# Another order for a hand-scheduled kernel: first loads on SyncE's queue, first weights on ScalarE's, and the rest of the instruction order searched anew

## The chip, the cores and the metric

The kernel runs on one core of a Trainium2 chip. The metric is the device time of one execution in microseconds (us). A "fast" run is one within 1.5% of the fastest run of the same kernel. Engines are named as the profile names them: PE is TensorE's matmuls, PEld its weight loads, DVE is VectorE, ACT is ScalarE, POOL is GpSimd, SP is SyncE, which here only issues DMAs. "L1085" is line 1085 of the kernel.

## The reference, cut to what matters

Two branches share x (2048 rows, 640 columns) and are mixed by a gate:

```python
def _A_ref(x, wq, wk, wv, wo, beta):      # 32 heads of 20, four segments of 512 rows
    q, k, v = heads(x @ wq), heads(x @ wk), heads(x @ wv)
    phi = lambda t: jnp.where(t > 0, t + 1.0, jnp.exp(t))
    for s in range(4):
        p = softmax(qs @ ks.T * scale + causal_mask)
        a_dot = p @ vs
        a_mem = (phi(qs) @ M) / (phi(qs) @ z + 1e-06)
        outs.append(g * a_mem + (1.0 - g) * a_dot)
        M, z = M + phi(ks).T @ vs, z + phi(ks).sum()
    return concat(outs) @ wo
def _B_ref(x, w_r, w_i):                  # spectral filter: rfft2, times W, irfft2
    return irfft2(rfft2(x) * (w_r + 1j * w_i))
g = sigmoid((x * gate_w).sum(-1, keepdims=True))
return g * a + (1 - g) * b
```

(The head reshapes and the loop's set-up are cut.) The Fourier transforms are matmuls with tables in the kernel, so TensorE carries both branches.

## The kernel before: what the change and the argument touch

The kernel builds a list of operations. A constant named ORDER then says in which order they are issued and on which engine each one goes. Every entry is twice the number of an operation, plus one if the operation runs on its second choice of engine:

```python
def schedule(self, pools, order, nsem=56):
    ops = self.ops
    queue = {e: [] for e in self.eng}
    for v in order:
        o = ops[v // 2]
        o.eng = list(o.alts)[v % 2]
        queue[o.eng].append(o)
    ...
ORDER = (
    47, 0, 90, 26, 74, 23, 2, 4, 37, 24, 6, 8, 28, 10, 12, 72, 14, 16, 30, 18, 20, 178, ...   # 2328 entries
```

So each engine has one fixed queue. An entry whose input is late holds up all that stand behind it on that engine, needed or not (one case, shown below, cost TensorE 2.15 us). The loads at the front are DMAs on the queues of SyncE or ScalarE; `EARLY` names those that may go on either:

```python
queues = ("sp", "act") if name in self.EARLY else (queue,)
```

The feature map phi is two VectorE operations between SBUF tiles, at L1084 and L1085 of the profile:

```python
fmax = lambda e: e.tensor_scalar(dst(), qsl(), 0.0, 1.0, ALU.max, ALU.add)
fmin = lambda e: e.tensor_tensor(dst(), dst(), et.ap(0, [1, L]), ALU.min)
```

The causal mask is GpSimd's (`affine_select`, L1284). The spectral product is read out of PSUM by VectorE (`W_mul`, Pt, L1439), and what follows it, an addition between SBUF tiles (`W_add`, Yt, L1444), may go on VectorE or GpSimd:

```python
def either(self, fn, n, r, w, prio, name="", after=()):
    return self.Sc.op({"dve": (fn, 67 + 0.52 * n, 68.0), "pool": (fn, 120 + 1.95 * n, 50.0)}, ..., lock=True)
```

In this kernel TensorE writes its results to PSUM, and another engine reads them out of there into SBUF. Such a read is called an evacuation below; TensorE waits for it before it writes the same bank of PSUM again.

TensorE works in three tilings: whole (128 x 128), in 32-column pieces and in small tiles for the scores (qkp). A change from one to another is called a change of mode.

The softmax here doesn't subtract the row's maximum and nothing guards it: scores larger than these inputs give would overflow.

## Time and profile before

| | before |
|---|---|
| median of 3 runs | 244.76 us (243.39 to 249.08) |
| span of the profiled run (an execution of its own, 246.77 us) | 244.7 us |
| TensorE busy | 94% of the span |
| VectorE / ScalarE / GpSimd busy | 81% / 81% / 68% |
| matmuls | 4361 (the trace holds 4347 of them) |

A row of the view of instruction groups reads: line, engine, operation, output<-input, size, count; then busy us in total and the mean of one in ns; then the idle time before them and its cause. This is a row of before that also belongs here, the second half of phi for q:

```profile
L1085 DVE TENSOR_TENSOR phq<-phq,et 128x512 bf16<-128x512 bf16 x15 | 6.7, 456 | 0.0
```

Keep its mean of 456 ns. The shortest of the 15 takes 407 ns and eleven of them at most 421, so in before most of them run undisturbed.

### The profile page before, as it was taken

The page shows a single profiled execution, that of the slowest core. Times are in us where ns is not written, and L with a number is a line of the kernel's source. Part 1 is how long each engine was busy: PE and PEld are TensorE (multiplying, and loading weights), DVE is VectorE, ACT ScalarE, POOL GpSimd, SP SyncE. Part 2 cuts the span into 40 slices and gives each one's busy share as a digit, 9 for nine tenths or more (in the row PEclk, how much of TensorE's full clock was granted, in tenths as well). Part 3 has the DMA queues.
Part 4 walks back from the last instruction along what each step waited for, and adds up shares of the span by engine and source line. Part 5 has one row for each costly group of instructions (what it writes and reads, how often), then busy time and mean ns, then how long its engine had stood idle before and what let it go on. Part 6 is the DMA issues. An engine that isn't in the chain of part 4 may idle for free.

```text
span 244.7 us, 10242 instructions
## 1 busy us (share of the span) xinstructions
PE 229.2 (94%) x4347; PEld 141.3 (58%) x4361; DVE 197.3 (81%) x481; ACT 199.3 (81%) x241; POOL 166.5 (68%) x297
## 2 busy tenths in 40 slices
PE   7699999999989999999889999899989999899994
PEld 2476566765556565555546555455545556467794
DVE  0379998879899996898899798998988878635563
ACT  2089688889899999999889979999899978388730
POOL 8514259447959956938964999877899867459730
PEclk9999999999999999999999999999999999599999
DMA  7999859993998775494688571264676995722123
GB/s 174 297 348 206 198 165 175 288 195 100 169 285 175 169 220 147 100 240 89 224 211 250 151 233 50 99 175 138 183 221 198 237 180 101 112 54 86 56 85 108
DMA packets 58928, 42.17 MB, mean 172 GB/s; under 512 B 30020, under 2 KB 55172, under 8 KB 58884
## 3 DMA queue, kind: packets, MB, share of 16 engines
q1 hardware_dynamic: 56100, 39.72, 66.4%
q10 hardware_dynamic: 2784, 1.81, 2.9%
q8 instruction: 34, 0.56, 1.0%
q14 instruction: 10, 0.08, 0.1%
HBM read 23.32 MB, written 12.30 MB: 146 GB/s over the span
## 4 chain that ended last, share of the span: by engine, by line
PE 59%; DVE 14%; DMA 10%; ACT 9%; SPq 3%; issue 2%; ACTq 0%; DVEq 0%
PE psum L514 53%; PE psum L512 7%; ACT ex L1263 6%; DMA xT<-in_A_x_dram 3%; DMA pkn<-phk 2%; SPq L548 2%; DMA r<-r_scr 2%; DVE Pt L1439 2%; DMA qk_scr<-qu 2%; DMA r_scr<-rc 2%; SPq L546 1%; DVE G L1485 1%; DVE phk L1085 1%; DVE oU L1526 1%; ACT et L1072 1%
## 5 line engine op out<-in xcount | busy, mean ns | idle before, releaser
L1284 POOL TENSOR_SCALAR_AFFINE_SELECT ex<-ex 128x256 bf16<-128x256 bf16 (+2 forms) x224 | 122.1, 567 | 41.1 <-ACT ex L1263 37.7
L1263 ACT ACTIVATE ex<-psum 128x2048 bf16<-128x2048 f32 (+4 forms) x92 | 138.7, 1508 | 13.9 <-PE psum L514 12.0
L514 PE MATMUL psum<-qkp 20*64 20x64 bf16 (+5 forms) x1280 | 32.7, 272 | 2.2 <-ACT ex L1263 1.7
L514 PE MATMUL psum<-xT,wk 128*128 128x256 bf16 (+1 forms) x280 | 34.1, 276 | 0.2 <-issue 0.2
L514 PE MATMUL psum<-wv,xT 128*32 128x321 bf16 (+3 forms) x400 | 30.1, 301 | 0.6 <-DVE va L1115 0.3
L514 PE MATMUL psum<-xT,wq 128*128 128x512 bf16 (+1 forms) x121 | 27.5, 396 | 2.6 <-DMA xT<-in_A_x_dram 2.0
L1439 DVE TENSOR_TENSOR Pt<-psum,Wt 128x642 bf16<-128x642 f32 x32 | 25.5, 821 | 2.3 <-PE psum L514 2.1
L514 PEld LDWEIGHTS psum<-qkp 20*64 20x64 bf16 x1280 | 13.5, 103 | 19.5 <-ACT ex L1263 13.6
L514 PEld LDWEIGHTS psum<-xT,wk 128*128 128x128 bf16 (+1 forms) x280 | 20.1, 99 | 6.4 <-issue 0.8
L512 PE MATMUL psum<-wo,oU 128*32 128x320 bf16 x480 | 23.5, 319 | 0.0
L906 POOL TENSOR_TENSOR xsb<-xf 128x320 bf16<-128x320 bf16 (+2 forms) x12 | 9.3, 777 | 17.7 <-DVE xsb L906 13.3
L525 DVE CAST ot<-psum 128x320 bf16<-128x320 f32 x21 | 10.1, 491 | 12.6 <-PE psum L512 10.1
L514 PEld LDWEIGHTS psum<-wv,xT 128*32 128x32 bf16 (+1 forms) x400 | 14.3, 96 | 8.4 <-issue 3.1
L514 PE MATMUL psum<-big,Ac 128*128 128x160 bf16 (+2 forms) x96 | 18.1, 258 | 0.7 <-DVE Pt L1439 0.3
L1115 DVE TENSOR_TENSOR va<-psum,ebx 128x320 bf16<-128x320 f32 x32 | 15.2, 484 | 4.3 <-ACT gate L1113 2.1
L514 PE MATMUL psum<-big,Cp 128*128 128x321 bf16 (+1 forms) x96 | 18.0, 302 | 0.2 <-DVE G L1485 0.2
L514 PE MATMUL psum<-ex,va 128*32 128x64 bf16 (+3 forms) x576 | 17.4, 256 | 0.7 <-DVE dn L1152 0.3
L1485 DVE TENSOR_TENSOR G<-eo,psum 128x320 bf16<-128x320 f32 x32 | 14.7, 482 | 3.6 <-PE psum L514 2.6
L514 PEld LDWEIGHTS psum<-ex,va 128*32 128x32 bf16 x576 | 11.1, 96 | 9.7 <-POOL ex L1284 3.4
L514 PE MATMUL psum<-tt,Yt 128*128 128x256 bf16 (+1 forms) x96 | 16.4, 275 | 0.2
L1072 ACT ACTIVATE et<-qu 128x512 bf16<-128x512 bf16 x25 | 15.6, 629 | 0.1
L512 PEld LDWEIGHTS psum<-wo,oU 128*32 128x32 bf16 x480 | 12.6, 101 | 5.3 <-issue 1.3
(99 smaller groups left out, 393.5 us busy)
## 6 DMA issues: line engine op xcount, KB each, us to landing
qkp<-qk_scr SPq DMA_DIRECT2D x28, 160.0 KB
tt<-tab_tt SPq DMA_DIRECT2D x8, 512.0 KB, 4.3
qk_scr<-qu SPq DMA_DIRECT2D x12, 256.0 KB, 3.1
u_scr<-ub SPq DMA_DIRECT2D x12, 256.0 KB, 3.8
xsb<-in_A_x_dram SPq DMA_DIRECT2D x6, 320.0 KB, 6.3
oU<-u_scr SPq DMA_DIRECT2D x15, 128.0 KB, 2.7
out_dram<-ot SPq DMA_DIRECT2D x12, 160.0 KB
Wt<-in_B_w_r_dram SPq DMA_DIRECT2D x16, 80.2 KB, 2.6
```

Of the source, the lines that this page charges most:

```text
L512: h = e.matmul(dst, wt, r_, start=st, stop=sp_, **{**kw, "tile_position": (0, q), "skip_group_check": True})
L514: h = e.matmul(o_, l_, r_, start=st, stop=sp_, **kw)
L525: alts["dve"] = (lambda e: e.tensor_copy(dst(), src()), 67 + 1.04 * n, 68.0)
L546: return e.dma_start_transpose(d_, s_)
L548: return e.dma_start(d_, s_)
L906: self.either(lambda e, dst=dst, src=src, d0=d0, n=n, op=op: e.tensor_tensor(xs.ap(o + dst, [D, 2], [1, n]), xf.ap(src + d0, [321, 2], [1, ...
L1072: self.one("act", lambda e: e.activation(et.ap(0, [1, L]), qsl(), ACT.Exp), L, [qb], [b("et", pi_)], late, name="phi_exp")
L1115: self.one("dve", lambda e: e.tensor_tensor(va.ap(i * H * VW + h0 * VW, [VW, nh], [1, DH]), self.ps(bank, 0, [DH, nh], [1, DH]), self.ebx. ...
L1263: self.one("act", lambda e, d=d, q=q: e.activation(self.ex.ap(*d), self.ps(bank, *q), ACT.Exp, scale=SC), n, [bank], [self.exb(s, 2 * pr + ...
L1284: self.one("pool", lambda e: e.affine_select(self.ex.ap(e0 + d0, [1280, 4], [1, n], np_=np_), self.ex.ap(e0 + s0, [1280, 4], [1, n], np_=np_),
L1439: self.one("dve", lambda e, ri=ri, Pt=Pt, Wt=Wt, wo_=wo_, bank=bank: e.tensor_tensor(Pt.ap(ri * 322, [644, 2], [1, KD]), self.ps(bank, 0, ...
L1485: self.one("dve", lambda e, q=q, n2=n2, bank=bank, eo=eo: e.tensor_tensor(self.G.ap(n2 * D + 639 * q, [1 - 2 * q, 320]), eo.ap(q, [1, 320] ...
```

## The change

The intent: put the first transposed chunks of x at the head of SyncE's queue with nothing on ScalarE's queue to compete, put the first weights on ScalarE's, and search the order of everything for a short time from scratch with measured durations of the transfers and of the ports. The diff touches no operation. Its core (the other lines of ORDER are cut; 2202 of the 2328 operations change their place in the list, half of them by six places or more, and 122 operations change engine or queue):

```diff
-    EARLY = ("ld_wqa", "ld_wka", "ld_wqb", "ld_wkb", "ld_wv", "ld_x", "ld_fcat", "ld_big", "ld_beta", "ld_gw", "ld_hm")
+    EARLY = ("ld_wqa", "ld_wka")
-        ... ("xT", 131072): (1260.0, 900.0, 16), ("xT", 262144): (1800.0, 1600.0, 16),
+        ... ("xT", 131072): (1240.0, 1300.0, 16), ("xT", 262144): (1700.0, 2300.0, 16),
     ORDER = (
-        47, 0, 90, 26, 74, 23, 2, 4, 37, 24, 6, 8, 28, 10, 12, 72, 14, 16, 30, 18, 20, 178, 64, 35, 202, ...
+        23, 0, 72, 28, 2, 4, 6, 26, 8, 10, 12, 76, 74, 36, 14, 46, 16, 24, 18, 30, 90, 44, 178, 64, 34, ...
```

In words: ScalarE's queue, which held a block of x (47), the first wq (23), beta (37), the rest of wk (35), another block of x and the gate column, keeps the first wq alone. SyncE's queue is now the transposed chunks 1-2 (28), chunk 0 (26), beta (36), a block of x (46), the first wk (24), the transposed chunks 3-4 (30), a block of x (44), the rest of wk (34). One of ten dummy matmuls that warm TensorE up moves behind the first wk work.

## The prediction

> **What bounds the kernel now.** I read the busy totals first, then the slices, then the timeline of TensorE wherever it was idle.
>
> ```profile
> span 244.7 us, 10242 instructions
> PE 229.2 (94%) x4347; PEld 141.3 (58%) x4361; DVE 197.3 (81%) x481; ACT 199.3 (81%) x241; POOL 166.5 (68%) x297
> ...
> PE   7699999999989999999889999899989999899994
> ```
>
> TensorE has work in flight for 229.2 of 244.7 us, so an order can win at most the 15.5 us of gaps, plus whatever is lost inside the busy share. The window table puts 3.3 us of the gaps before 12 us, 3.2 after 235 us (the last stores, which no order removes) and the other 9 in between, mostly pieces of 0.2 to 0.5 us. Two places are larger. The first is in the start:
>
> ```profile
> start us, us, engine line op out<-in xcount [idle before <-releaser]
> 4.69 1.06 PE L514 MATMUL psum<-G 128*128 128x512 bf16 x2
> 5.70 1.05 PE L514 MATMUL psum<-xT,wq 128*32 128x512 bf16 x8
> 7.63 0.40 PE L514 MATMUL psum<-xT,wq 128*32 128x512 bf16 x4 [0.28 <-DMA xT<-in_A_x_dram]
> ...
> 9.16 0.39 PE L514 MATMUL psum<-xT,wk 128*32 128x256 bf16 x8
> 11.25 0.40 PE L514 MATMUL psum<-xT,wq 128*32 128x512 bf16 x4 [1.70 <-DMA xT<-in_A_x_dram]
> ```
>
> Ten dummy matmuls on G fill 1.3 to 5.7 us, then the first projection waits for transposed chunks of x: 0.28 us for chunks 1 and 2, and 1.70 us for chunks 3 and 4. That last transpose was issued at 4.45 us and the chain shows 6.75 us from there to its landing:
>
> ```profile
> 4.45 6.75 DMA xT<-in_A_x_dram
> ```
>
> The second place is late, and it carries a penalty behind it:
>
> ```profile
> 207.34 0.25 PE L514 MATMUL psum<-va,ex 128*128 128x21 bf16 x4
> 209.04 0.46 PE L514 MATMUL psum<-G,fbg 128*32 128x320 bf16 x4 [1.46 <-DVE on L1325]
> ...
> 206.00:208.00 2.00, 1.58 (x58) 1.26 (x42) 1.97 (x5) 1.69 (x2) 1.60 (x2) 1.00 1.11 119
> 208.00:210.00 2.00, 0.96 (x16) 0.63 (x20) 1.93 (x6) 0.36 (x1) 0.28 (x2) 0.58 0.19 39
> 210.00:212.00 2.00, 2.00 (x56) 1.00 (x48) 1.11 (x3) 1.11 (x3) 0.80 (x2) 0.50 0.61 163
> ```
>
> In the last three rows the third number from the right is the granted clock: after the 1.46 us gap it falls to 0.50. The clock record in the trace gives 208.3 to 215.2 us, 6.8 us at half speed.
>
> **What the Trainium skill says.** "Perfetto Trace Analysis", section Identifying the Most-Contended Engine, warns that matmul busy time is not a measure of how full TensorE is. The trace agrees: the columns streamed by all matmuls, at the full-clock step the trace shows (0.107 us for 256 columns), sum to 188 us, 41 less than "busy". "TensorEngine Tiling (Array Packing)", Key Properties, says that changing the tiling mode drains TensorE. The trace shows the cost:
>
> ```profile
> 13.10 1.26 PE L514 MATMUL psum<-xT,wk 128*128 128x256 bf16 x10
> 14.30 0.43 PE L514 MATMUL psum<-qkp 20*64 20x512 bf16 x12
> 14.66 3.23 PE L514 MATMUL psum<-xT,wk 128*128 128x256 bf16 x28
> 17.82 0.42 PE L514 MATMUL psum<-qkp 20*64 20x320 bf16 x16
> ```
>
> Ten matmuls of 256 columns at 0.107 us end at 14.17, the next mode starts at 14.30; 28 of them end at 17.66, the next starts at 17.82. So 0.13 to 0.16 us per change of mode. "DMA: Bandwidth & Descriptors", Queues, rings and completion order, says that each engine takes turns between the queues with work, and that a completion increment lands only after all earlier writes of that engine, across its queues. The trace agrees: nearly all packets of chunks 3 and 4 had gone by 8 us, when the ACT queue's second half of wk and a block of x began to flow:
>
> ```profile
> q10 hardware_dynamic: 790, 0.90, 91.2%
> q1 hardware_dynamic: 487, 0.16, 18.7%
> ```
>
> That is 7.5 to 11.2 us; q10 is ACT's queue, q1 SyncE's. The transpose's increments arrived at 9.8 to 11.2 us, the competing wk at 10.7 to 11.0. "TensorE: Matmul & The Clock Gate", Part 1, says that the clock is halved after a mostly idle window of about 3.4 us and restored after a busy one; the 6.8 us spell is two such windows, and the first matmuls above take 0.427 us per 512 columns (cold) until about 7 us, 0.213 after.
>
> **The change, part by part.** No arithmetic is added or removed: 4361 matmuls in both; DVE has 482 instructions for 481, GpSimd 300 for 301, and ACT computes as often as before.
>
> 1. Start. The ACT queue keeps only the first slice of wq; it loses five DMAs (two blocks of x, beta, the rest of wk, the gate column). SyncE's queue becomes: chunks 1-2, chunk 0, beta, x, first wk, chunks 3-4, x, rest of wk. With the issue times of the trace (1.75 us for two chunks, 1.24 for one, 0.4 to 0.6 for a plain load) chunk 0 is issued by 3.85 us instead of 2.02; packets started about 1.0 us after the end of an issue and landing followed the last packet by 0.85, so I estimate chunk 0 at 6.1 us, against 5.6. Nine dummies end at 5.15, so the first real matmul starts 0.4 us later than now. The x block (0.9 us of transfer) then precedes the first wk, which I put at 8.2 us instead of 6.4: about 1 us of waiting once 16 wq matmuls are done. Chunks 3-4, issued by 7.2 us with nothing on the other queue, land near 10.0 instead of 11.2, before they are needed. From 8.3 us TensorE still has 16 of 20 groups of 0.213 us, one dummy (0.43) and its two mode changes (0.3): 4.1 us, end near 12.4 where the direct projection now ends at 13.1. But the rest of wk, behind another x block, needs about 1.0 + 2.2 us of transfer after 9.2 us and lands at 12.9 to 13.1. Net: -0.1 us, with -0.7 to +1 possible.
>
> 2. Mode changes. Counted over the two compiled orders, TensorE changes mode 229 times before and 245 times after. Sixteen more at 0.11 to 0.15 us (the lower from the median step over all changes) is +1.8 to +2.4; some will fall on a wait that exists anyway. I count +1.6.
>
> 3. The late wait. Before, DVE ran five multiplications by r as soon as r came back from DRAM at 204.5 (2.14 us), then a reciprocal pair, then an addition that took 1.5 us, and only then the evacuation (L1325) that TensorE waited for. In the new order that addition stands behind the evacuation: 1.5 us earlier relative to r. And by stream time and mode changes TensorE reaches this point 0.9 us later after the last flipped product of the third segment (23.2 against 22.3 us). Both together exceed 1.46: I expect the gap to go, -1.4. If it goes, the half clock behind it can go too: at most 3.4 us, about 2.5 since drains do not scale with the clock. I give that one half: -1.2.
>
> 4. Remaining order: 9 us of small gaps, dealt anew. No sign known: 0, give or take 2.
>
> 5. Early clock. Dummies stop at 5.15 and TensorE then waits twice for about 1 us, so the clock may rise a window later; much of that is hidden under the wait for wk. +0.4.
>
> Sum: -0.1 + 1.6 - 1.4 - 1.2 + 0.4 = -0.7, hence 244.76 - 0.7 = 244.1. I round toward no change, since a short search from cold has no claim to fewer small gaps: 244.5 us.
>
> **Rivals.** (a) The start is bound by transfers, not by the queue: all SyncE loads now stand in one line, so wk, wv and the table of the first transform land no sooner and the projection only waits elsewhere. For it: the DMA row is nearly full up to 30 us. Against it: the 1.70 us wait was a completion held back by the other queue. It makes +0.5 to +1.5 at the start, 246 in all. (b) More mode changes and a new set of stalls dominate: +2.4 and no late gain, since r still takes a store of 4.05 us and a load of 4.66 us; 247. A second halved window at a new place would add another 2.5 to 3: 249. (c) Late gap and half clock both vanish and the start gives 0.7: 240.5. The runs of before spread from 243.4 to 249.1, so such a clock spell may come and go between runs; that speaks against reading a single figure too finely.
>
> **Range and chances.** Two percent is 4.9 us. To be faster than 239.9 needs the full late gain, the start's best case and mode changes hidden: 0.08. To be slower than 249.7 needs a worse start, all mode changes exposed and a further clock spell: 0.09. Within 2%: 0.83. The range of 8 in 10 is 240.8 to 248.5.
>
> **What would show it.** Right: chunks 3-4 off the path, a wait for wk (first near 7 to 8 us, then near 12.5), the first real matmul near 6.1, the end of the direct projection within 0.7 us of 13.1; about 16 more short drains; no gap over 1 us between the last Cp product and the last projection; granted clock of 1.00 from 205 to 235. Wrong: TensorE still waiting for xT at 9 us or later; the first four waits summing to much more than 3.3 us; the gap at L1325 still there; or halved clock slices in the middle of the run, which would mean a new stall that I did not foresee.

## The result, and the profile after

| | before | after |
|---|---|---|
| median, same rounds, 4 runs each | 246.55 us (243.39 to 249.08; of the four, 248.33 and 249.08 are slow) | 253.75 us (252.87 to 254.54) |
| ratio of fast runs, 95% interval | | 1.0389 (1.0342 to 1.0436) |
| span of the profiled run | 244.7 us | 252.7 us |
| mean granted clock of the profiled run | 0.986 | 0.986 |

Ratios, here and below, are taken from fast runs alone, of both kernels in the same rounds, so they are not the ratio of the medians beside them. The change made the kernel 3.9% slower. That is not a matter of the clock: both profiled runs were granted 0.986 on average.

The first view of after is its page: the totals, then the granted clock in 40 slices, in tenths. The same clock row of before's page stands below it.

```profile
span 252.7 us, 10265 instructions
PE 233.0 (92%) x4361; PEld 140.3 (56%) x4361; DVE 205.2 (81%) x482; ACT 200.9 (79%) x241; POOL 167.8 (66%) x296
...
PEclk9679999999999999999999999999999999999999
```

```profile
PEclk9999999999999999999999999999999999599999
```

VectorE is busy 205.2 us for 197.3 before, with one instruction more and the same arithmetic. The clock row has its dip at the start (6 and 7 in slices 2 and 3) and none late; before had none early and a 5 in slice 35.

TensorE's timeline shows the start. A line is: start, duration, engine, line, operation, count, and in brackets the idle time before and what ended it.

```profile
5.85 1.05 PE L514 MATMUL psum<-xT,wq 128*32 128x512 bf16 x16 [0.63 <-DMA xT<-in_A_x_dram]
9.43 1.04 PE L514 MATMUL psum<-xT,wk 128*32 128x256 bf16 x16 [2.53 <-DMA wk<-in_A_wk_dram]
...
11.77 2.35 PE L514 MATMUL psum<-xT,wk 128*32 128x256 bf16 x40
```

The wait for wk is 2.53 us. The window table (the third number from the right is the granted clock) says what follows it:

```profile
10.00:12.00 2.00, 2.00 (x29) 0.57 (x21) 1.15 (x2) 0.00 (x0) 1.84 (x3) 0.50 1.08 321
12.00:14.00 2.00, 2.00 (x44) 1.49 (x40) 0.90 (x1) 0.00 (x0) 0.63 (x2) 0.50 1.06 356
```

Half clock, in the record from 8.4 to 15.2 us, just where the first projection runs. The same table at the place of before's late gap:

```profile
208.00:210.00 2.00, 2.00 (x44) 0.92 (x43) 2.00 (x5) 1.72 (x3) 2.00 (x5) 1.00 0.50 149
210.00:212.00 2.00, 2.00 (x58) 1.07 (x56) 0.54 (x2) 1.50 (x3) 2.00 (x4) 1.00 0.47 121
```

Full clock and a busy TensorE: what the prediction hoped for late came about. The loss lies between. The row that answers to the one shown of before:

```profile
L1085 DVE TENSOR_TENSOR phq<-phq,et 128x512 bf16<-128x512 bf16 x15 | 12.5, 834 | 0.0
```

The same 15 operations now take 834 ns in the mean instead of 456. The costliest single case, from the timelines of TensorE, VectorE and GpSimd in turn:

```profile
152.54 0.24 PE L514 MATMUL psum<-big,Ac 128*128 128x161 bf16 x1 [2.15 <-DVE Pt L1439]
...
148.98 2.77 DVE L1085 TENSOR_TENSOR phq<-phq,et 128x512 bf16<-128x512 bf16 x1
151.67 0.82 DVE L1439 TENSOR_TENSOR Pt<-psum,Wt 128x642 bf16<-128x642 f32 x1
...
149.19 0.47 POOL L1361 TENSOR_TENSOR Mz<-Macc,hm 128x154 bf16<-128x154 f32 x1
149.62 0.45 POOL L1284 TENSOR_SCALAR_AFFINE_SELECT ex<-ex 128x256 bf16<-128x256 bf16 x1
150.06 1.41 POOL L1444 TENSOR_TENSOR Yt<-Pt 128x321 bf16<-128x321 bf16 x2
```

Read it from the bottom. GpSimd runs four operations without a pause from 149.19 to 151.47. VectorE's phi operation, issued at 148.98, is on record for 2.77 us instead of some 0.41 and ends soon after, before the next mask (which started at 151.42) is done. Behind it in VectorE's queue stands Pt, which frees the PSUM bank that TensorE waits for, so TensorE stands still for 2.15 us. The Trainium skill has this in "SBUF — State Buffer", section SBUF: two separate sides: VectorE and GpSimd share a pair of ports that is "an exclusive lock, not a bandwidth split". The trace agrees with that, with these numbers.

To add the loss up, I matched the trace's weight loads to the compiled order and took from TensorE's time the time that its columns need at full clock (187.9 us in both kernels). What is left (waits, drains, half clock) is 51.9 us before and 59.9 after. By the amount of column work done so far, with the number of stretches of one mode beside it:

| us of column work done | before: us lost (stretches) | after: us lost (stretches) | difference |
|---|---|---|---|
| 0 to 8 (start) | 5.7 (5) | 8.7 (6) | +3.0 |
| 8 to 30 | 2.1 (12) | 2.3 (16) | +0.2 |
| 30 to 150 (middle) | 34.3 (170) | 41.7 (173) | +7.4 |
| 150 to 188 (late) | 9.8 (43) | 7.3 (51) | -2.5 |
| all | 51.9 (230) | 59.9 (246) | +8.0 |

### The profile page after: what moved, and what is told of

Read it like the earlier page. It is cut to its first block, busy times and chain, and to the rows that moved or that the text cites. A ratio compares the mean times of both kernels' runs of the same rounds, so it can differ in the third digit from the quotient of the medians.

```text
span 252.7 us, 10265 instructions
## 1 busy us (share of the span) xinstructions
PE 233.0 (92%) x4361; PEld 140.3 (56%) x4361; DVE 205.2 (81%) x482; ACT 200.9 (79%) x241; POOL 167.8 (66%) x296
## 4 chain that ended last, share of the span: by engine, by line
PE 61%; DVE 15%; ACT 14%; issue 3%; DMA 2%; POOL 2%; SPq 1%; DVEq 0%
PE psum L514 55%; ACT ex L1263 10%; PE psum L512 6%; DVE Pt L1439 3%; DVE phq L1085 2%; DMA wk<-in_A_wk_dram 2%; POOL ex L1284 2%; DVE phq L1084 2%; ACT et L1072 1%; DVE G L1485 1%; SPq L546 1%; DVE ub L525 1%; ACT Cp L523 1%; DVE Yt L1444 1%; ACT ub L523 1%
## 5 line engine op out<-in xcount | busy, mean ns | idle before, releaser
L514 PE MATMUL psum<-xT,wq 128*128 128x512 bf16 (+1 forms) x135 | 31.7, 409 | 1.1 <-DMA xT<-in_A_x_dram 0.6
L514 PE MATMUL psum<-wv,xT 128*32 128x320 bf16 (+3 forms) x400 | 29.8, 301 | 1.5 <-DVE va L1115 1.5
L512 PE MATMUL psum<-wo,oU 128*32 128x320 bf16 x480 | 22.5, 301 | 0.0
L906 POOL TENSOR_TENSOR xsb<-xf 128x322 bf16<-128x322 bf16 (+2 forms) x12 | 9.9, 834 | 16.9 <-DVE xf L901 9.9
L514 PE MATMUL psum<-big,Ac 128*128 128x161 bf16 (+2 forms) x96 | 18.4, 257 | 2.7 <-DVE Pt L1439 2.1
L514 PE MATMUL psum<-big,Cp 128*128 128x321 bf16 (+1 forms) x96 | 18.6, 303 | 0.4 <-DVE G L1485 0.2
L525 DVE CAST ot<-psum 128x320 bf16<-128x320 f32 x23 | 10.8, 488 | 8.2 <-PE psum L512 3.8
L514 PEld LDWEIGHTS psum<-ex,va 128*32 128x32 bf16 x576 | 11.4, 96 | 10.7 <-POOL ex L1284 3.8
L514 PE MATMUL psum<-Bt,tt 128*128 128x321 bf16 x64 | 13.8, 304 | 1.3 <-DVE Pt L1439 0.7
```

Of the source, the lines that this page charges most:

```text
L512: h = e.matmul(dst, wt, r_, start=st, stop=sp_, **{**kw, "tile_position": (0, q), "skip_group_check": True})
L514: h = e.matmul(o_, l_, r_, start=st, stop=sp_, **kw)
L525: alts["dve"] = (lambda e: e.tensor_copy(dst(), src()), 67 + 1.04 * n, 68.0)
L906: self.either(lambda e, dst=dst, src=src, d0=d0, n=n, op=op: e.tensor_tensor(xs.ap(o + dst, [D, 2], [1, n]), xf.ap(src + d0, [321, 2], [1, ...
```

## The experiments

My theory after the result: the larger part is the middle, where VectorE's SBUF operations wait for GpSimd in front of evacuations that TensorE needs. The rival: the start is late and half-clocked, and all that comes after is a consequence of it. A third: the 16 further changes of mode cost far more than the 0.1 us that I counted. All kernels gave correct results.

**Start and middle crossed.** Two kernels are made by cutting one order at the end of the first projection and going on with the other: h_start takes before's start and after's rest, h_rest the opposite.

```diff
 # h_start (in terms of after)
-    ORDER = after[:all]            EARLY = ("ld_wqa", "ld_wka")
+    ORDER = before[:end of first projection] + (after without these)   EARLY = as in before
 # h_rest (in terms of before)
-    ORDER = before[:all]
+    ORDER = after[:end of first projection] + (before without these)
```

> Hybrid: the loads and all work up to the end of the direct projection in the order and queues of the kernel before, everything else in the order of the changed kernel. If the losses add (the new order is worse in the middle by itself): 3 us less than the changed kernel, 250 to 250.8, with the middle stalls on DVE still there. If the middle loss is a consequence of the late start (plan and machine out of step): near 245, within 1 us of the kernel before.

> The start and the loads of the kernel after, then the order of the kernel before for the rest: the complement of h_start. If the middle's order is the larger part of the loss (my theory): +0.5 us over before where the start's clock is not halved and +3 where it is, so a ratio of 1.002 to 1.012. If the loss came from the start and everything later is its consequence: 1.03 or more as in the kernel after.

| | before's rest | after's rest |
|---|---|---|
| before's start | 246.55 (fast runs 243.39 and 244.76) | h_start 254.6 (254.02 to 255.05), ratio 1.0369 [1.0275, 1.0464] |
| after's start | h_rest 246.45 (245.11 to 247.03), ratio 1.0029 [0.997, 1.0089] | 253.75, ratio 1.0389 |

The rest decides and the start hardly shows in the total. (The rest is the middle and the late part; the late part of after is the better one, so it is the middle that loses.) That settles the rival: the loss in the middle is not a consequence of the start. The row of phi goes with the order too, here in h_start and then in h_rest:

```profile
L1085 DVE TENSOR_TENSOR phq<-phq,et 128x512 bf16<-128x512 bf16 x15 | 12.3, 820 | 0.0
```

```profile
L1085 DVE TENSOR_TENSOR phq<-phq,et 128x512 bf16<-128x512 bf16 x15 | 6.6, 453 | 0.0
```

In h_rest's profile TensorE is 2.8 us late after the start and keeps just that lag, between 2.0 and 2.8 us, until 160 us of column work are done, and it loses 33.8 us in the middle for before's 34.3. It then wins the lag back, because in that run no halved clock followed the late gap of 1.54 us. The wait of its start, from TensorE's timeline:

```profile
8.80 1.05 PE L514 MATMUL psum<-xT,wk 128*32 128x256 bf16 x16 [2.09 <-DMA wk<-in_A_wk_dram]
```

In h_start's profile the start is 3.3 us earlier than after's, but the middle loses 42.1 us; part of that is a halved clock of 3.41 us right behind a gap of 2.20 us at 148.6.

**The start mended within after.** In a_wk_act the first wk goes to ScalarE's queue, behind wq. In a_dummies TensorE runs a tenth dummy before the first real work and seven more during the wait for wk, to keep the clock up.

```diff
 # a_wk_act
-        23, 0, 72, 28, ... 16, 24, 18, 30, ...
+        23, 25, 0, 72, 28, ... 16, 18, 30, ...
 # a_dummies
+    seven more "warm" matmuls of 512 columns ahead of the first wk matmuls; the tenth dummy (20) back beside the ninth (18)
```

> The changed kernel with one edit: the first slice of wk goes out on ACT's queue, right behind the first slice of wq. Theory S (the late first wk opens a 2.53 us wait, and the clock halves after it): wk lands near 5 us instead of 9.4, the 2.53 us gap goes, the clock record has no half-speed spell after 7 us, the direct projection ends near 13.1 instead of 16.2, and the whole run is about 3 us shorter, near 250.5. Rival R (the start is bound by the bytes on the DMA engines, so the wait moves to the second half of wk or to the transposed x): direct projection still ends at 15 us or later and the run stays within 1 us of 253.7.

> The changed kernel with dummy matmuls in its waits: the tenth dummy put back before the first projection, and seven more between the wq groups and the first wk group. The wait for wk itself stays. If the half clock is what costs most of the start: clock at 1.00 from about 8 us on, no half-speed spell until the end, first transform matmul about 2 to 3 us earlier than 21.25, run about 2.5 us shorter (251). If the wait alone costs it: no gain beyond 0.5 us, or a small loss.

a_wk_act took 252.92 us (252.23 to 253.6), ratio 1.0302 [1.0205, 1.0399]; a_dummies 253.04 (251.69 to 253.53), ratio 1.0298 [1.0194, 1.0403]. The wait for wk is gone from the profile of a_wk_act and it runs 2.8 us ahead of after, with the lead constant as far as 147 us. Then it is spent. The same gap as in after now was followed by a half clock, and a second wait appears at the end (TensorE's timeline, and the window table between the two):

```profile
149.79 0.24 PE L514 MATMUL psum<-big,Ac 128*128 128x161 bf16 x1 [2.20 <-DVE Pt L1439]
...
152.00:154.00 2.00, 2.00 (x24) 0.87 (x22) 1.83 (x5) 0.92 (x1) 2.00 (x3) 0.50 0.71 184
...
223.95 0.32 PE L514 MATMUL psum<-G,fbg 128*32 128x320 bf16 x4 [0.89 <-DVE ot L525]
```

So in the profile 1.0 us of the lead went to the clock and 0.97 to the late wait. In that wait an evacuation (ot) stands in VectorE's queue behind an addition (L1534) whose input is still in flight by DMA. A start that is 2.8 us better was worth some 1 us at the end. a_dummies tells the same: 2.9 us ahead at the start (the same work compared), half clock from 150.7 for 3.41 us, 1.0 ahead at the end. It also says what the start of after is made of. Its first wk landed at 8.73 us and that work began at 9.12 instead of 9.43, but dummies had filled the wait, the clock stayed full and the first projection was over at 13.2 us instead of 16.2. So the half clock, and not the wait itself, is most of after's +3.0 there.

**VectorE's queue.** a_swap moves phi steps of after, at three places, behind evacuations that TensorE waits for. In a_yt_dve two Yt additions go from GpSimd to VectorE, which shortens GpSimd's run around 150 us.

```diff
 # a_swap: places in ORDER
-    phi_max 1940, 1920 ahead of the evacuation va 2176
+    va 2176, then phi_max 1940, 1920
-    phi_min 3306 ahead of W_mul 1338;  phi_min 3348 ahead of W_mul 1390
+    W_mul 1338, then phi_min 3306;  W_mul 1390, then phi_min 3348
 # a_yt_dve: engine of two entries
-    1431, 1433      (W_add on GpSimd)
+    1430, 1432      (W_add on VectorE)
```

> The changed kernel with three moves in DVE's queue and nothing else: at three places (near 42, 133 and 149 us) the operations on phq that stood in front of a PSUM evacuation and took 1.0 to 2.8 us instead of 0.23 to 0.36 are put behind that evacuation. Theory Q (what the new order loses in the middle is DVE's queue blocked in front of evacuations while GpSimd holds the memory port): the TensorE gaps of 1.47 us at 43.8 and 2.15 us at 150.4 go, phq operations stay stretched somewhere, run shorter by 2.5 to 4 us, 250 to 251. Rival M (the middle loss is the 16 extra changes of tiling mode and small waits everywhere): less than 1 us.

> The changed kernel with the two additions into Yt that GpSimd ran at 150.06 to 151.47 us given to DVE instead. If the 2.77 us of the phq minimum at 148.98 is a wait for GpSimd to let go of the port: it shortens by about 1.4 us, to 1.3, and the 2.15 us gap shrinks to about 0.8. If the DVE operation is slow for another reason: still 2.5 us or more.

a_swap: 250.09 us (249.88 to 250.29), ratio 1.0174 [1.0111, 1.0237], so about 3.7 us less than after by the medians. Its profile had no halved clock at the start, which is worth 2.6 us and has nothing to do with the moves; the moves themselves show as 0.7 us at 43 us, 0.7 at 133 and 1.7 at 150, and 0.97 goes back to the late wait of 0.89 us. In the accounting the middle loses 38.6 us for after's 41.7, and that is what the moves are worth. That the total met the 2.5 to 4 us expected is in part luck: the start's full clock is more of it than the moves less what the late wait took back. a_yt_dve: 251.19 us. Its timelines at the place shown above (TensorE, VectorE, GpSimd):

```profile
148.25 0.24 PE L514 MATMUL psum<-big,Ac 128*128 128x161 bf16 x1 [0.78 <-DVE Pt L1439]
...
146.05 1.40 DVE L1085 TENSOR_TENSOR phq<-phq,et 128x512 bf16<-128x512 bf16 x1
...
146.31 0.47 POOL L1361 TENSOR_TENSOR Mz<-Macc,hm 128x154 bf16<-128x154 f32 x1
146.74 1.03 POOL L1284 TENSOR_SCALAR_AFFINE_SELECT ex<-ex 128x256 bf16<-128x256 bf16 x2
```

With the 1.41 us of Yt gone from GpSimd's run, the phi operation is 1.37 us shorter (1.40 for 2.77) and TensorE's wait 1.37 us shorter (0.78 for 2.15). The phi operation, its input and what stands before it on VectorE are the same; only what GpSimd did meanwhile is not. That shows the cause of 1.37 us of this gap, and one execution is all there is of it. The other 0.78 us was not taken apart: phi still takes 1.40 us for 0.41, while GpSimd runs from 146.31 on without a pause. The time of the run also owes something to its start, which was not half-clocked either.

**Changes of mode.** b_modes is before with a dummy matmul of 64 columns in a 32-column tile between the two matmuls of each of the 32 spectral products, so 64 more changes of mode. b_modes0 has the same dummies untiled.

```diff
+                def dm(ri=ri, tt=tt, to=to, Bt=Bt, bank=bank):
+                    return (self.ps(bank, 448, [1, 64], np_=32), tt.ap(to + 2 * ri * P, [1, 32]), Bt.ap(0, [1, 64]), False, True, {"tile_position": (0, 0), ...})
+                items.insert(1, (dm, 0))
 # b_modes0: np_=128, [1, 128] and no tile_position
```

> The kernel before with a tiled 32-column dummy matmul of 64 columns between the two matmuls of each of the 32 T operations: up to 64 more changes of tiling mode and nothing else moved. If a change of mode costs the 0.14 us that the accounting of the traces gives (median excess of one change, both kernels), it comes out 64 x 0.141 = 9 us longer than its untiled control, less what falls into gaps in which TensorE would have waited anyway: 6 to 9 us. If a change costs the 0.1 us that the prediction counted: 6 us at most, 4 to 6. If mode changes were free and the excess only sat beside them, it is level with the control within 1 us.

> The control of b_modes: the same 32 dummies of 64 columns untiled (128 x 128), so no change of mode. Both theories: 32 x about 0.03 us of columns and the weight load beside it, +1 to +2 us over the kernel before.

The medians, 250.83 and 250.41 us, look as if a change of mode were free. They can't be compared: three of the four runs of b_modes0 had a mean clock of 0.973 to 0.979 (in the profiled one, a halved clock of 10.2 us behind a late gap of 1.66), and only one had 0.999. The clock rows of the two pages, b_modes first:

```profile
PEclk9999999999999999999999999999999999999999
```

```profile
PEclk9999999999999999999999999999999997589999
```

At equal clock there are three runs of b_modes at 1.0 (251.32, 249.66, 250.34, mean 250.44) and one of b_modes0 at 0.999 (243.56): 6.9 us for 64 changes, 0.108 us each. The traces agree. Between 30 and 130 us of column work, with full clock in both, b_modes loses 32.1 us in 198 stretches and the control 25.1 in 133: 7.0 over 65, 0.108. This is the stronger of the two figures: the difference of the times rests on one fast run of the control, and the profiled run of b_modes also lost some 1.5 us more at its start, in a wait for x of 3.38 us for 1.87. So a change of mode costs 0.11 us where it is added alone; the 0.14 that I had taken from the median excess of a stretch, and expected here, is too much, and the control's expected +1 to +2 us was a miss too: at full clock its 243.56 is no longer than before's 243.9 at 1.0 in the same rounds. Sixteen further changes are thus 1.7 us. The third theory falls.

**The late part alone.** h_late is before as far as 193 us, then after.

```diff
-    ORDER = before[:all]
+    ORDER = before[:late part] + (after without these)
```

> Hybrid: the kernel before up to about four fifths of its work (near 193 us), then the changed kernel's order. If the changed kernel's late part is better by itself (no 1.46 us gap behind L1325, no half clock after it): 241 to 242, about 3.5 us less than the kernel before when that one has the half-clock spell. If the late gain came from the different state at hand-over: within 1 us of the kernel before, or slower by a seam of 1 us.

245.45 us (244.58 to 246.74), ratio 0.9986 [0.9866, 1.0106]. In its profile the late gap of 1.46 us and the half clock behind it are gone, and from 150 to 165 us of column work it loses 4.6 us for 7.5. It does not show in the times of these rounds. In the profiled run the start had a gap of 2.44 us and a half clock instead, and runs of before at full clock never pay for the late one at all: its 11 runs of one batch go from 243.9 (clock 1.0) to 248.37 (0.986).

**A version that beats both?** b_start2 gives before a new order of the first loads (wq, wk, a block of x and beta on ScalarE's queue; the transposed chunks 0, 1-2, 3-4 on SyncE's). best1 adds the late part of after. best2 then delays the block of x and moves two entries in VectorE's queue; best3 is best1 with one of these two, the late addition (L1534) moved behind the two evacuations that it blocked.

```diff
 # b_start2 (in terms of before)
-        47, 0, 90, 26, 74, 23, 2, 4, 37, 24, 6, 8, 28, ... 30, ... 35, ... 45, 42, ...
+        23, 25, 0, 90, 26, 74, 47, 2, 4, 37, 6, 8, 28, ... 30, ... 34, ... 44, 42, ...
 # best1: + after's late part
 # best2: 47 later, 37 three places earlier; addmem 4322 behind the evacuation 4385; phi_max 3304 later
 # best3: best1 with addmem 4322 behind 4385
```

> The kernel before with another order of its first loads: ACT's queue has the first slices of wq and wk, then beta and one block of x; SyncE's has the three transposes of x one after the other, then the rest of wk and the blocks of x. If a transposed chunk is held back by the other queue's traffic only while that queue has work: chunks 3-4 land by 8.5 us, the 1.70 us gap goes, the direct projection ends near 11.4 instead of 13.1, and the run is 1.5 us shorter if nothing later takes it back. If bytes bind: the projection then waits for the rest of wk until 12.5 and the gain is under 0.7 us.

> The loads of b_start2, the middle of the kernel before, and the late part of the changed kernel (the earlier hybrid with a new start). If gains add: 1.5 us at the start and 3.5 us late against a run of the kernel before that has the half-clock spell, so 240 to 242. If one of them is given back: 243 to 245.

> The kernel before with the new loads, but the block of x on ACT's queue is issued after ACT's first activation so that the rows of c for chunks 1 and 2 land ahead of it; the middle of before; the late part of after; and two vector operations moved back in DVE's queue (the memory addition that waited for a DMA late, 0.89 us of gap in the run best1; the phi maximum). If waits ahead of TensorE are what the time is made of: the gap of 1.35 us at 6.9 us goes (-1), the late gap of 0.89 us goes (-0.9), so 242 to 243 us and a ratio near 0.985. If a start that is earlier is only given back by later waits or by a halved clock, it stays at the 0.994 of best1.

> The run best1 with one more move: the late memory addition, which waits for a DMA, behind the two evacuations that it blocked in VectorE's queue. If TensorE's gap of 0.89 us near 213 us is worth its length: 0.9 us less than best1, so a ratio to before of 0.990. If what is behind it waits anyway: the 0.994 of best1.

| | median (range), runs | ratio to before |
|---|---|---|
| b_start2 | 244.14 us (243.93 to 245.79), 4 | 0.9947 [0.9878, 1.0016] |
| best1 | 244.35 us (244.15 to 244.77), 4 | 0.9944 [0.987, 1.0018] |
| best2 | 246.38 us (244.45 to 246.75), 6 | 1.0013 [0.9955, 1.0071] |
| best3 | 243.77 us (242.69 to 244.57), 6 | 0.9955 [0.9893, 1.0016] |

In b_start2's profile chunks 3-4 landed at 8.82 us instead of 11.21 and the first projection was over at 11.8 instead of 13.1, as expected if the other queue's traffic had held them back. TensorE now waited 1.35 us for chunks 1-2 (8.17 us for 7.58), and the late gap (1.76 us) and the half clock of 6.8 us about it were there as in before. So the gain at the start shows in the profile and not beyond doubt in the times. best1 lost the late half clock as well and yet came out at 244.35, not at the 240 to 242 expected if gains add.

best2 was a miss. With the block of x later, what depends on it came later on GpSimd, then on VectorE, whose queue in turn held the evacuation that TensorE needed (TensorE, then VectorE):

```profile
15.41 0.43 PE L514 MATMUL psum<-qkp 20*64 20x512 bf16 x12 [3.29 <-DVE qkp L525]
...
12.98 0.49 DVE L901 TENSOR_TENSOR xf<-xsb 128x640 bf16<-128x640 bf16 x1 [5.82 <-POOL xf L901]
```

In best3's profile the late gap is gone and the late part is 1.1 us shorter than in best1's; the 0.990 expected lies in the interval, but so does the 0.994 of the rival. By fast runs alone none of the four is shown to be faster than before. What best3 does show is steadiness: clocks of 0.993 to 1.0 in all six runs, none above 244.57, where the 11 runs of before beside it have a median of 245.96 and reach 249.02, with four slow (clocks of 0.979 to 0.986).

**All repairs of after at once.** a_all has the moves of a_wk_act and a_swap and the late addition of best3.

```diff
+    a_wk_act's 25 behind 23;  a_swap's three moves;  addmem 4322 behind 4385
```

> The kernel after with four repairs at once: the first block of wk on ACT's queue, the three moves in VectorE's queue of a_swap, and the late memory addition behind the two evacuations that it blocked. If the repairs add once their gains are no longer given back: 3.7 us of a_swap, up to 2.5 of the start (less where a run of a_swap already had no halved clock), 0.9 of the late wait, so about 247 us, a ratio of 1.004 to 1.010. If gains at the start are taken up by the next wait whatever is done: it stays at the 1.017 of a_swap.

248.84 us (248.22 to 249.69), ratio 1.0164 [1.011, 1.0219]. That is 1.2 us less than a_swap by the medians, though the two ratios, taken against different rounds of before, don't tell them apart. The sum that I had expected (247) is not reached. Its clock was full in all six runs, so no half clock hides in it. Compared with before's profile, the start loses 0.2 us less, the late part 2.5 less, and the middle 38.4 us for 34.3. These 4.1 us are not explained by one place: within the middle a_all has 55 steps from one matmul to the next that take over 0.3 us more than the columns need, before has 45, and the sums are 24.3 and 18.7 us. They are small waits spread over the middle, 51 of the 55 where one kind of product follows another, and I did not take them apart. The stretched phi operations are not all gone either: counting those at L1084 and L1085 that take at least 0.3 us more than the shortest of their kind, before has 6 (3.1 us in excess in all), h_rest 6 (3.4), after 15 (11.3), h_start 16 (11.4), and a_all still 13 (7.4). What those 13 cost TensorE was not tested.

## Why the prediction was wrong

- **Step 1, the start (-0.1), with step 5, the early clock (+0.4).** Chunk 0 landed at 5.71 us (I said 6.1), chunks 3-4 at 10.41 (10.0), the rest of wk at 13.35 (12.9 to 13.1). All near, and so chunks 3-4 did leave the path. The first wk was late: 9.38 us instead of 8.2, and a wait of 2.53 instead of about 1. TensorE was idle for 2.1 of the 3.4 us before 8.4 (0.63 before the first wq work, the rest of the wait up to then), and the first projection ran at half clock: it ended at 16.17 us instead of 12.4 to 13.1. Both terms together were +0.3; the profile has +3.0. Of the two, step 5 is the one that was mis-sized: a_dummies, with the first wk no earlier than 8.73 us but full clock, ended the projection at 13.2, and the same start in a_swap without the half clock lost 2.6 us less. So the clock cost some 2.6 us for the +0.4 counted, and the longer wait little, since the rest of wk landed at 13.0 to 13.4 in any case. ("TensorE: Matmul & The Clock Gate", Part 1, speaks of an idle window of about 3.4 us; "mostly idle" in the prediction was my reading of a 1.46 us gap, and not the page's.) What I wrote as the sign of being wrong ("the first four waits summing to much more than 3.3 us") was not what came: two waits of 3.2 us in all, and the clock on top. In the 2 x 2 of start and rest, though, the start is worth under 1 us in the total, for it is given back or made up for at later clock windows.
- **Step 2, sixteen further changes of mode (+1.6).** Right: 16 at 0.108 us are 1.7.
- **Step 3, the late wait and the half clock behind it (-1.4 and -1.2).** Right in the mechanism and nearly in the size: the gap and the half clock are gone, 2.5 us less lost in the late part of after (2.9 between 150 and 165). The half clock itself was put at about 2.5 us; the late part of h_rest, which had a gap of 1.54 us and full clock, lost some 2.6 us less than that of before. My halving of the clock term was a guess at how often it occurs, and the runs of before, at clocks from 0.979 to 1.0, say that it does vary from run to run.
- **Step 4, "Remaining order: 9 us of small gaps, dealt anew. No sign known: 0, give or take 2."** This is the step that failed: +7.4 us in the middle. Two things were wrong in it. The sign was knowable: I did say that a short search from cold "has no claim to fewer small gaps", but a random deal of an order that was tuned for long can hardly come out even, so its centre belonged above zero. (That is an argument; no run tests other deals.) And its size was bounded by TensorE's gaps alone; I had not asked which queued operations of VectorE stand between GpSimd's long runs and an evacuation. Phi operations on VectorE that were stretched by 0.3 us or more went from 6 (3.1 us) to 15 (11.3 us). h_start and h_rest show that the order of the middle is the cause, a_swap that three moves of such operations are worth about 3 us of the middle's 7.4, a_yt_dve, at one place, that GpSimd's run is what the operation waits for. The other 4 us are placed in the middle's order, but their single causes stay open.
- **The rivals.** (b) came nearest in kind, "a new set of stalls", but I gave it 247, and 249 with a new halved window: the stalls alone were larger than that. (a), a start bound by transfers, shows in the wait for wk; that the start came out at +3.0 and not at +0.5 to +1.5 is mostly the half clock.

## What to carry to other kernels

In a kernel with one fixed queue per engine, a new order of 2200 instructions is not neutral noise: ask, for each evacuation that the busiest engine needs, what stands in front of it in its queue and what that one waits for, a lock, a DMA or another engine. When only a part of a new order is wanted, cross the old and the new at a seam: four runs told here what no sum of waits could. And compare times at equal clock, for of a gain of 2.8 us at the start one was lost to a half clock behind a gap of 2.2 us that at other times had full clock behind it.

## What the Trainium skill lacked or had wrong

- "TensorE: Matmul & The Clock Gate", Why this matters for your kernels, advises no idle gaps over some 3 us between bursts. Here gaps of 1.46 us (before, late), 2.53 (after, start) and 2.2 (a_wk_act, middle) each came with 3.4 or 6.8 us at half clock that began within the gap or up to 0.9 us after it. And the length of the gap does not decide: the same gap of 2.15 us in after and 2.20 in a_wk_act was followed by full clock in the one and half clock in the other, and one of 3.38 us in b_modes (9.6 to 13.0 us) by full clock. Windows whose phase differs from run to run would explain it; no run here sets that phase.
- The same page does not say what this does to a comparison: runs of the kernel before at mean clocks of 1.0 and 0.979 in one batch took 243.9 and 248.14 us, and the two kernels of the mode experiment seemed equal (250.83 and 250.41) that differ by 6.9 us at equal clock (one run of the control).
- "TensorEngine Tiling (Array Packing)", Key Properties, says that a change of mode drains TensorE but gives no cost: 0.108 us each here.
- "SBUF — State Buffer", SBUF: two separate sides, says that the loser of the ports waits for the whole instruction of the other. Here it waited longer than for one: a phi operation of 0.41 us was on record for 2.77 us, through four back-to-back operations of GpSimd.
- No page looked up says what a load costs behind others on one DMA queue: the first wk took 4.8 us from its issue to its landing as the fifth on SyncE's queue in after (4.57 to 9.38), and 3.9 us as the second on ScalarE's in best3 (1.26 to 5.18).
